# A new account of tiling changes in a kernel's planner, a freer place for eight scalings, and a refitted order: windowed attention followed by a four-expert mixture

## The chip, the cores and the metric

The kernel runs on one core of one Trainium2 chip. A core has five engines that run their own streams of instructions: TensorE (PE in the profile; its weight loads are listed as PEld), VectorE (DVE), ScalarE (ACT), GpSimd (POOL) and SyncE (SP). The metric is the device time of one execution in microseconds (us). Three runs of the kernel before took 358.85, 358.95 and 359.42 us; the median is 358.95.

## The reference

First an attention with "sink" keys and a short window: every query sees the first four keys and the 128 keys that end at itself. Then a mixture of four experts, each a pair of matrix products, weighted by normalised probabilities of the token.

```python
B, H, S, D = 4, 8, 768, 64          # n_sink 4, window 128
scores = scale * np.matmul(q, k.transpose(0, 1, 3, 2))
rel = pos[:, None] - pos[None, :]
keep = (pos[None, :] < n_sink) | ((rel >= 0) & (rel < window))
scores = np.where(keep, scores, -1000000000.0)
a = np.exp(scores - np.max(scores, axis=-1, keepdims=True))
a = a / (np.sum(a, axis=-1, keepdims=True) + 1e-09)
x = np.matmul(a, v).transpose(0, 2, 1, 3).reshape(B * S, H * D)   # 3072 x 512

p = domain_probs / (domain_probs.sum(-1, keepdims=True) + 1e-09)  # 3072 x 4
for e in range(4):                  # w1[e] 512 x 1024, w2[e] 1024 x 512
    h = np.maximum(x @ w1[e], 0.0)
    out += p[:, e:e + 1] * (h @ w2[e])
```

## The kernel before

**Attention.** Operands of TensorE are bf16, sums fp32 in PSUM. The four batches `b` are cut into three output groups `g` of 256 tokens and four pairs of heads `hp`. For a group, L706 makes the scores of a pair of heads (keys on the partitions, only the blocks inside the window), ACT takes the exponential into `aT` (L746), DVE multiplies by the window's mask (L754 in the first batch, L727 later; for `g` 0 of the first batch the mask is added in PSUM by products with `low` instead, L700). The sink keys' scores are L667, of 32 rows each. L779 (sinks) and L786 (window) multiply by the values into a PSUM tile `od` of 65 columns per head, the last of them the sum of the weights. DVE takes its reciprocal `R` (L813), and `od` times `R` is written to `onat`. For the first batch DVE does that in one instruction of 256 columns (L816); for the later batches ACT does it in four of 64 columns (L825, `multiply`). A bank of PSUM that holds `od` comes free when this is done.

The mixture needs tokens on the columns, so `onat` is turned to `xT`: by TensorE and a copy for the first batch (`turn`, L847), by one transposing DMA on SP's queue per group later (L803), issued behind the last of the group's four scalings. Rows of q and k are turned to `qkT` by TensorE in the first batch (L595, L598, copies L302) and by transposing DMAs on SP (L281) later. POOL issues the loads of rows (L271), values (L331) and weights.

**Mixture.** The first two groups of the first batch (`DENSE`) are done plainly: L1106 for `x @ w1` and L1433 for the second product, each collected by DVE with the gate as a column. All other groups save products: both matrix products are split into two by two blocks and done with seven block products instead of eight, so sums of operands and of results come in. For the first product these are

- `T`: four differences of blocks of `xT`, made by DVE in `tokens` (L1158), one after the other, each put off to a later place by a slack in ns;
- four forms of each expert's `w1` and `w2` (`weight_form1`, `weight_form`, L369 to L410), also DVE's;
- seven products P1, P5, P6, P2, P7, P3, P4 of 8 matmuls of 128 columns (L1189, `emit_fast`), whose PSUM tiles are copied, added to and finished by ACT and DVE (L1232, L1239, L1245, L1254), ending in `gated` (L1223), which takes relu and multiplies by a row of gates. P1 starts two PSUM tiles; where the second has not been wholly written since its last use as another shape (`unset`), a matmul of 512 columns writes it first.

The second product goes through the same seven (`CHAIN`), 4 matmuls of 256 columns for each expert and product (L1358, `emit_product`), with sums `S` of `H` (DVE, as `chore`), into two accumulator banks. After P1 its bank is copied to the other accumulator by ACT (L1387); DVE and ACT collect the rest into `osb` (L1390 to L1405), which SP stores.

The gates as rows are made once in `gates_by_row` (L462 to L468: four small DVE operations and a store to a tile in DRAM, `gate_rows`); `load_gate` (L485) broadcasts a row of it to all partitions. The planner places this when its clock passes `GROW`.

**The order.** Nothing reorders the instructions on the chip; the Python program that writes the kernel plans the order. It keeps a clock `t` for each engine, advanced by modelled costs (`pe`, `act`, `dve`, `pool`, `sp`), and a time at which each of six PSUM banks comes free. In the main loop it lists what PE could do next (a step of attention, a first product, a second product, a dense one), with the time each is ready and a priority number, and emits one. Work for DVE and ACT is put in a list by `later(engine, ready, slack, run)`; `flush` gives a free engine, among the entries that are ready, the one with the earliest due time (ready plus slack). An entry marked "any" goes to DVE or ACT, whichever the clock has free first. Where the clock sees PE without work for more than 220 ns, `idle_products` (L574) fills in a matmul of 256 columns of zeros. The constants at the top (`SHARE_OF`, `LEAD`, `LOW_PRODUCT`, `GATE`, `FORM`, `TOKEN` and so on) are slacks, priorities and the pace at which a later batch's attention is mixed into the experts' products. The modelled cost of a PE step has 95 ns for a change between tile sizes of the array: before, two such changes (`switch=2`) are charged to each step that uses small tiles, at its start, whatever came before or comes after.

Of the kernel before, what the change touches and what calls it, by code (L numbers as in the profile page):

```python
# [16 lines left out]
def kernel(  # L17
# [12 lines left out]
    nc = tc.nc  # L30

    B, H, S, D = q.shape
# [5 lines left out]
    P = 128  # L38
# [23 lines left out]
    DENSE = 2  # L62
    NT3 = 3
    MIX = 4
    SHARE_OF = (0.634, 1.111, 1.102)
    LEAD = (1.272, 0.235)
    DUE = 0
    LOW_PRODUCT = 2.791
    LOW_SECOND = 4.402
    HIGH_PRODUCT = 0.207  # L70
    EARLY = 0.154
    GATE = 8921
    GATE0 = 5401
    FORM = 20576
    FORM2 = 37391
    TOKEN00 = 33179
    TOKEN0 = 1119
    WAIT2 = 16164
    WAIT1 = 5898
    LATE3 = 3  # L80
    TOKEN = 11155
    MARGIN = 494
    FULL = 7
    STEP0 = 0.141
    READY = 46
    WIDE = 2
    OPEN = 1.198
    ONACT = 1
    ONE = 2
    PAIR = 1  # L90
    SINK2 = 1
    PAD = 198
    MASKD = 99999999
    GROW = 24662
    ONLY2 = 1
    BEHIND = 7198
    CHORES = 2
    OWN = 2
    BIASED = 1
    FAST = tuple(START)  # L100
# [7 lines left out]
    t = {"pe": 1200.0, "act": 0.0, "dve": 0.0, "pool": 1280.0, "sp": 800.0, "sw": 6500.0, "hw": 0.0}  # L108
    ring, whole = [0.0] * 6, [False] * 6
    WARM = 6600.0  # L110
    FLIP = 421
    LATE = 259
    LATE1 = 12449

    def pe(cols, *deps, n=1, switch=0):
        t["pe"] = max([t["pe"], *deps])
        rate = 2.4 if t["pe"] > WARM else 1.2
        t["pe"] += cols / rate + 2.5 * n + 95 * switch
        return t["pe"] + 215

    def act(cols, *deps):
# [41 lines left out]
    def later(engine, ready, slack, run):  # L163

        pend.append((ready, ready + slack, engine, run))
# [80 lines left out]
    qkn_free, scored_at = [0.0] * NQB, {}  # L246
# [334 lines left out]
    def transposes(b, g, hp):  # L581

        if b not in qkT:
            qkT[b] = sb.tile([P, 2, NHP, S], BF16, name="qkT", tag="qkT", bufs=1)
        ready = max(cast_at[hp // 2] if (b, g) == (0, 0) else rows_at(b, g), free_at(2 if (b, g) == (0, 0) else 1))
        slots, trs = [], []
        for i in range(2 if (b, g) == (0, 0) else 1):
            slots.append(pick())
            trs.append(bank(slots[i], [P, 2, 2, P], BF16, "tr"))
            ring[slots[i]] = 1e12  # L590
        hs = slice(2 * hp, 2 * hp + 2)
        for i in range(2):
            for tt in range(2):
                if (b, g) == (0, 0):
                    nc.tensor.transpose(trs[i][:, i, tt], first["qk"[i]][:, tt, hs], ident)  # L595
                    continue
                for ph in range(2):
                    nc.tensor.transpose(  # L598
                        trs[0][64 * ph:64 * ph + 64, i, tt], nat[b, 2 * g + i][:, 2 * hp + ph, tt * D:(tt + 1) * D], ident,
                    )  # L600
        done = pe(4 * P, ready, n=4, switch=0 if (b, g) == (0, 0) else 2)
        dst = qkT[b][:, :, hp, g * G:(g + 1) * G]

        def copied(at):
            for slot in slots:
                take(slot, at)
            turned_at[b, g, hp] = at

        if (b, g) == (0, 0):
            part = join(2, copied)  # L610
            for i, engine in enumerate(("dve", "act")):
                def run(engine, i=i):
                    copy(engine, dst[:, i].rearrange("c (p t) -> c p t", t=2), trs[i][:, i].rearrange("c t p -> c p t"))
                    part(clock(engine, 2 * P))
                later(engine, done, 0, run)
        else:
            def run(engine):
                copy(engine, dst.rearrange("c i (p t) -> c i p t", t=2), trs[0].rearrange("c i t p -> c i p t"))
                copied(clock(engine, 4 * P))
            later("any", done, 300, run)  # L620
        if hp == NHP - 1:
            for _ in range(2):
                qkn_free.remove(1e12)
                qkn_free.append(done)
            qkn_free.sort()
# [32 lines left out]
    def sinks(b, piece, n=1, joined=False):  # L658

        if b not in sinkA:  # L660
            sinkA[b] = sb.tile([P, 2 * G], BF16, name="sinkA", tag="sinkA", bufs=1)
        q0, q1 = piece * G, (piece + n) * G
        ready = 0.0 if joined else sinks_ready(b, piece, n)
        slot = pick()
        sp = bank(slot, [P, 2 * G], FP32, "sinks")
        for hp in range(NHP):
            nc.tensor.matmul(  # L667
                sp[32 * hp:32 * hp + 32, 0:q1 - q0], lhsT=ksd[b % 2][:, hp, :],
                rhs=qkT[b][:, 0, hp, q0:q1], start=True, stop=True,
            )  # L670
        done = pe(q1 - q0, 0.0 if joined else ready, switch=0 if joined else 2)
        ring[slot] = 1e12

        def run(engine):
            nc.scalar.activation(
                out=sinkA[b][:, q0 - G:q1 - G], in_=sp[:, 0:q1 - q0], func=AF.Exp, scale=scale,
            )
            at = act(q1 - q0)
            take(slot, at)
            for i in range(n):  # L680
                sinkA_at[b, piece + i] = at
        later("act", done, 800, run)
# [4 lines left out]
    def scores(b, hp, g, more=False):  # L687
        T = qkT[b]
        w = sum(x[2] for x in GROUPS[g]) * P
# [13 lines left out]
        for (kb, qb, nq) in GROUPS[g]:  # L703
# [6 lines left out]
                    start=not biased and c == 0, stop=True, skip_group_check=True,  # L710
                )
            c += nq * P
        scored_at[b] = done = pe(w, ready, n=6, switch=0 if more else 2)
        a = sb.tile([P, 2, w], BF16, name="aT", tag="aT", bufs=4)
        m = mask0 if g == 0 else mask1

# [46 lines left out]
    def values(b, hp, g):  # L763
# [33 lines left out]
        def scaled(at):  # L797
            take(slot, at)
            onat_at[b, hp, g] = at
            onat_n[b, g] = onat_n.get((b, g), 0) + 1  # L800
            if b and onat_n[b, g] == NHP:
                xT[b, g] = sb.tile([P, 2, NHP, P], BF16, name="xT", tag=home(b, g), bufs=1)
                nc.sync.dma_start(  # L803
                    out=xT[b, g].rearrange("c q h p -> c (q h) p"),
                    in_=o.rearrange("p q h c -> p (q h c)"), transpose=True,
                )
                turned_out = sp(at, issue=1330, takes=1400, turning=True)
                for x in range(NHP):
                    xT_at[b, x, g] = turned_out

        def run(engine):
            R = sb.tile([P, 2, 2, 1], FP32, name="R", tag="R", bufs=6)
            nc.vector.reciprocal(out=R, in_=od[:, :, :, D:DX])  # L813
            at = dve(4, fixed=171)
            if b < ONACT:
                nc.vector.tensor_mul(  # L816
                    o[:, :, hp].rearrange("p q (h d) -> p q h d", h=2), od[:, :, :, 0:D], R.to_broadcast([P, 2, 2, D]),
                )
                scaled(dve(2 * P))
                return  # L820

            def multiply(engine):
                for qi in range(2):
                    for ph in range(2):
                        nc.scalar.mul(o[:, qi, hp, ph * D:(ph + 1) * D], od[:, qi, ph, 0:D], R[:, qi, ph])  # L825
                        at = act(D)
                scaled(at)
            later("act", at, 600, multiply)
        later("dve", done, 500, run)
        values_at[b, g] = done  # L830

# [141 lines left out]
    class Mixture:  # L973
# [164 lines left out]
        def tokens(self):  # L1138

            pairs = [(b, g) for b in range(B) for g in range(NG) if any(self.is_fast(b, g, e) for e in FAST)]  # L1140
            n = len(self.T)
            if n == len(pairs):
                return
            b, g = pairs[n]
            if n >= NT3 and any((*pairs[n - NT3], e) not in self.finished for e in range(E)):
                return
            at = max(xT_at.get((b, hp, g), 1e12) for hp in range(NHP))
            if at > t["pe"] or t["pe"] < TOKEN00:
                return
            at = t["pe"]  # L1150
            x = xT[b, g]
            B11, B21, B12, B22 = x[:, 1, 0:2], x[:, 1, 2:4], x[:, 0, 0:2], x[:, 0, 2:4]
            T = sb.tile([P, 4, 2, P], BF16, name="T", tag="T", bufs=NT3)
            self.T[b, g] = {"P1": B11, "P2": B21, "P3": B22, "P4": T[:, 3], "P5": T[:, 0], "P6": T[:, 1], "P7": T[:, 2]}
            steps = [(T[:, 0], B12, B11), (T[:, 1], B22, T[:, 0]), (T[:, 2], B22, B12), (T[:, 3], B21, T[:, 1])]

            def run(engine):
                nc.vector.tensor_sub(*steps.pop(0))  # L1158
                done = dve(G, rate=1.92)
                if steps:  # L1160
                    later("dve", t["dve"], 1500 if b else TOKEN0, run)
                else:
                    self.T_at[b, g] = done
            later("dve", at, TOKEN if b else TOKEN0, run)

        def emit_fast(self, u, m, ready):
            b, g, e = u["unit"]
# [437 lines left out]
```

## Time and profile before

| | us | share of the span | instructions |
|---|---|---|---|
| profiled execution | 358.95 | | |
| its span | 357.2 | | 11108 |
| `cps` products, L1189, share of the chain | | 35% | |
| `acc` products, L1358, share of the chain | | 31% | |
| scalings L825 on ACT, busy | 32.8 | 9% | 144 |
| gated products L1223 on DVE, busy | 69.8 | 20% | 105 |
| exponentials L746 on ACT, busy | 46.5 | 13% | 96 |

The profiled execution took as long as the median of the three runs, so sums made against it can be read against the median. The span, 357.2 us, is the stretch in which the engines worked; 1.75 us of the time lie around it. Shares of the busy time don't tell which engine sets the end; the chain of waits (the work that ended last, followed back step by step) does. The engines' busy times overlap each other.

### The profile page before, as it was taken

How to read it: one execution, taken by the hardware profiler on the slowest of the kernel's cores; microseconds unless marked ns; L12 is line 12 of the kernel's file. 1: busy time of each engine (PE TensorE's matmuls, PEld its weight loads, DVE VectorE, ACT ScalarE, POOL GpSimd, SP SyncE). 2: the span in 40 equal slices, each digit the busy share in tenths (PEclk: the TensorE clock that was granted, in tenths of full speed). 3: DMA queues.
4: the chain of work that ended last, by engine and by line, in shares of the span. 5: the costliest groups of instructions: out<-in, count | busy, mean ns of one | idle time of the engine just before them, and what ended most of it. 6: DMA issues, size and time to landing. Idle time of an engine off the chain costs nothing.

```text
span 357.2 us, 11108 instructions
## 1 busy us (share of the span) xinstructions
PE 348.8 (98%) x4673; PEld 302.6 (85%) x4673; DVE 306.7 (86%) x701; ACT 168.7 (47%) x432; POOL 70.5 (20%) x90
## 2 busy tenths in 40 slices
PE   8999999999999999999999999999999999999995
PEld 3675687777688998998998998899899999999884
DVE  6669999998799899899699799699799699999630
ACT  5866451437882922566444722926443632322110
POOL 8934114311260440420030620000000000000000
PEclk9999999999999999999999999999999999999999
DMA  9999999999993999691086999124112221100011
GB/s 175 185 195 203 230 210 174 137 135 139 227 148 42 138 168 157 75 119 46 32 68 111 148 156 139 50 54 55 44 32 63 59 52 51 37 31 31 1 61 60
DMA packets 115318, 37.86 MB, mean 106 GB/s; under 512 B 97196, under 2 KB 110764, under 8 KB 115268
## 3 DMA queue, kind: packets, MB, share of 16 engines
q0 software_dynamic: 74416, 17.31, 55.4%
q1 hardware_dynamic: 39796, 19.32, 29.3%
q8 instruction: 36, 0.59, 0.7%
q10 hardware_dynamic: 1056, 0.52, 0.6%
q14 instruction: 14, 0.11, 0.1%
HBM read 41.03 MB, written 6.34 MB: 133 GB/s over the span
## 4 chain that ended last, share of the span: by engine, by line
PE 83%; DVE 6%; ACT 5%; DMA 2%; issue 1%; POOL 1%; DVEq 0%
PE cps L1189 35%; PE acc L1358 31%; PE acc L1433 7%; PE hps L1106 3%; PE sps L706 3%; ACT onat L825 2%; PE od L786 2%; ACT aT L746 2%; DMA vx<-in_v_dram 2%; DVE H L1223 1%; DVE cps L1239 1%; DMA gates<-gate_rows 1%; PE od L779 1%; DVE onat L816 1%; DVE H L1254 1%
## 5 line engine op out<-in xcount | busy, mean ns | idle before, releaser
L1189 PEld LDWEIGHTS <-w 128*128 128x128 bf16 x1408 | 87.1, 98 | 3.5 <-issue 1.0
L1358 PEld LDWEIGHTS <-H 128*128 128x128 bf16 x720 | 66.6, 98 | 7.9 <-issue 1.2
L1223 DVE SCALAR_TENSOR_TENSOR H<-cps,gates 128x512 bf16<-128x512 f32 x105 | 69.8, 683 | 0.0
L1358 PE MATMUL acc<-w,H 128*128 128x256 bf16 x432 | 56.8, 273 | 0.1
L1189 PE MATMUL cps<-xT,w 128*128 128x128 bf16 x704 | 52.5, 219 | 0.5 <-ACT onat L825 0.5
L1189 PE MATMUL cps<-T,w 128*128 128x128 bf16 x704 | 52.5, 219 | 0.1
L746 ACT ACTIVATE aT<-sps 128x512 bf16<-128x512 f32 (+1 forms) x96 | 46.5, 571 | 9.7 <-PE sps L706 9.5
L1232 ACT COPY cps<-cps 128x512 f32<-128x512 f32 x44 | 25.7, 592 | 44.2 <-PE cps L1189 33.8
L1405 ACT COPY osb<-acc 128x256 f32<-128x256 f32 x40 | 15.4, 384 | 59.2 <-PE acc L1358 59.2
L825 ACT ACTIVATE onat<-od,R 128x64 bf16<-128x64 f32 x144 | 32.8, 349 | 21.7 <-DVE R L813 21.7
L1358 PE MATMUL acc<-wf,H 128*128 128x256 bf16 x288 | 39.3, 273 | 0.0
L1189 PEld LDWEIGHTS <-qkn 128*128 128x128 bf16 x576 | 34.8, 98 | 1.1 <-issue 0.2
L1239 DVE TENSOR_TENSOR cps<-H,cps 128x512 f32<-128x512 f32 x40 | 27.7, 691 | 9.0 <-PE cps L1189 6.2
L1358 PEld LDWEIGHTS <-S 128*128 128x128 bf16 x320 | 30.2, 98 | 4.2 <-issue 1.0
L1245 ACT COPY H<-cps 128x512 f32<-128x512 f32 x40 | 23.7, 600 | 18.1 <-PE cps L1189 18.1
L1433 PE MATMUL acc<-w,H 128*128 128x512 bf16 x128 | 30.1, 379 | 0.0
L1189 PEld LDWEIGHTS <-vf 128*128 128x128 bf16 x480 | 28.8, 98 | 0.1
L331 POOL DMA_DIRECT2D vx<-in_v_dram x24 | 21.4, 909 | 37.4 <-PE od L786 25.9
L1254 DVE TENSOR_TENSOR H<-H,cps 128x512 f32<-128x512 f32 x40 | 27.0, 680 | 1.7 <-PE cps L1189 1.6
L271 POOL DMA_DIRECT2D rows<-in_q_dram x18 | 16.0, 887 | 61.1 <-DMA qkT<-rows 51.0
L1189 PE MATMUL cps<-T,qkn 128*128 128x128 bf16 x384 | 27.3, 219 | 0.1
L727 DVE TENSOR_TENSOR aT<-aT,mask 128x1024 bf16<-128x1024 bf16 (+1 forms) x36 | 22.8, 641 | 1.9 <-ACT aT L746 1.6
(123 smaller groups left out, 524.2 us busy)
## 6 DMA issues: line engine op xcount, KB each, us to landing
w<-in_moe_w_dram POOLq DMA_DIRECT2D x7, 1024.0 KB, 23.1
out_dram<-osb SPq DMA_DIRECT2D x23, 256.0 KB
gates<-gate_rows SPq DMA_DIRECT2D x40, 128.0 KB
vx<-in_v_dram POOLq DMA_DIRECT2D x24, 128.0 KB, 10.0
rows<-in_q_dram POOLq DMA_DIRECT2D x18, 128.0 KB, 6.4
rows<-in_k_dram POOLq DMA_DIRECT2D x18, 128.0 KB, 6.7
w<-in_moe_w_dram POOLq DMA_DIRECT2D x4, 256.0 KB, 8.4
kraw<-in_k_dram ACTq DMA_DIRECT2D x2, 256.0 KB
```

What stands on the lines that cost most here:

```text
L331: nc.gpsimd.dma_start(out=vx[tb][:, :, 0:D], in_=v[b, :, tb * P:(tb + 1) * P, :].rearrange("h p d -> p h d"),)
L727: nc.vector.tensor_mul(x, x, m[:, None, :].to_broadcast([P, n, 2 * w // n]))
L746: nc.scalar.activation(out=a[:, ph], in_=sps[ph][:, 0:w], func=AF.Exp, scale=scale)
L825: nc.scalar.mul(o[:, qi, hp, ph * D:(ph + 1) * D], od[:, qi, ph, 0:D], R[:, qi, ph])
L1189: nc.tensor.matmul(y[:, f], lhsT=A[:, d, f * P:(f + 1) * P], rhs=T[:, d], start=(m in ("P1", "P5") and f == 0 and d == 0), stop=(d == 1), ...
L1223: nc.vector.scalar_tensor_tensor(out=dst, in0=src, scalar=0.0, in1=gate, op0=ALU.max, op1=ALU.mult)
L1232: nc.scalar.copy(out=tiles["Y"], in_=y)
L1239: nc.vector.tensor_add(tiles["V"], c5, tiles["X"])
L1245: nc.scalar.copy(out=c5, in_=y)
L1254: nc.vector.tensor_add(c5, c5, y)
L1358: nc.tensor.matmul(x, lhsT=self.operand(b, g, e, m)[:, f], rhs=forms[e][m][:, f], start=(k == 0 and f == 0 and m in (("P1", "P5", "P2") if ...
L1433: nc.tensor.matmul(op, lhsT=H[:, fb // QF, fb % QF, s], rhs=w2_sb[e][:, fb, :], start=(fb == 0), stop=(fb == NFB - 1),)
```

## The change

The changed kernel computes the same thing. Four things are changed in the planner:

1. `pe` takes the number of rows of the step's tiles (128, 64, 65 for scores, 32 for sinks) and adds 95 ns where it differs from the step before. A tiling change is thus charged where it happens, also when a step of full tiles comes behind small ones, and not at all between steps of one kind.
2. For the second batch's first two output groups, (b, g) below `EITHER` = (1, 2), the scaling of `od` may run on DVE (as in the first batch, one instruction) or on ACT (four), whichever the clock has free first.
3. The four sums `T` of the second batch's first group get the slack `TOKEN1` (544 ns) instead of `TOKEN` (11155 ns) for the first and 1500 ns for the rest; and the time at which the planner believes that this group's `xT` has landed is at most `TURN1` (8645 ns) after its last scaling.
4. Some thirty constants have other values.

```diff
-    SHARE_OF = (0.634, 1.111, 1.102)
-    LEAD = (1.272, 0.235)
+    SHARE_OF = (0.909, 1.101, 1.118)
+    LEAD = (1.223, 0.045)
...
-    LOW_PRODUCT = 2.791
-    LOW_SECOND = 4.402
-    HIGH_PRODUCT = 0.207
-    EARLY = 0.154
-    GATE = 8921
-    GATE0 = 5401
-    FORM = 20576
-    FORM2 = 37391
-    TOKEN00 = 33179
-    TOKEN0 = 1119
-    WAIT2 = 16164
-    WAIT1 = 5898
+    LOW_PRODUCT = 2.173
+    LOW_SECOND = 3.131
+    HIGH_PRODUCT = 0
+    EARLY = 0.129
+    GATE = 6941
+    GATE0 = 7604
+    FORM = 13638
+    FORM2 = 49917
+    TOKEN00 = 25720
+    TOKEN1 = 544
+    TURN1 = 8645
+    TOKEN0 = 4051
+    WAIT2 = 15049
+    WAIT1 = 9563
     LATE3 = 3
-    TOKEN = 11155
-    MARGIN = 494
-    FULL = 7
-    STEP0 = 0.141
-    READY = 46
+    TOKEN = 13631
+    MARGIN = 0
+    FULL = 8
+    STEP0 = 0.122
+    READY = 0
     WIDE = 2
-    OPEN = 1.198
+    OPEN = 0.21
     ONACT = 1
+    EITHER = (1, 2)
...
-    PAD = 198
+    PAD = 208
     MASKD = 99999999
-    GROW = 24662
+    GROW = 32046
     ONLY2 = 1
-    BEHIND = 7198
-    CHORES = 2
+    BEHIND = 2768
+    CHORES = 1
...
-    FLIP = 421
-    LATE = 259
-    LATE1 = 12449
-
-    def pe(cols, *deps, n=1, switch=0):
-        t["pe"] = max([t["pe"], *deps])
+    FLIP = 809
+    LATE = 3730
+    LATE1 = 10389
+
+    tiling = [P]
+
+    def pe(cols, *deps, n=1, rows=P):
+        t["pe"] = max([t["pe"], *deps]) + 95 * (rows != tiling[0])
+        tiling[0] = rows
         rate = 2.4 if t["pe"] > WARM else 1.2
-        t["pe"] += cols / rate + 2.5 * n + 95 * switch
+        t["pe"] += cols / rate + 2.5 * n
         return t["pe"] + 215
...
-        done = pe(4 * P, ready, n=4, switch=0 if (b, g) == (0, 0) else 2)
+        done = pe(4 * P, ready, n=4, rows=P if (b, g) == (0, 0) else 64)
...
-        done = pe(q1 - q0, 0.0 if joined else ready, switch=0 if joined else 2)
+        done = pe(q1 - q0, 0.0 if joined else ready, rows=32)
...
-        scored_at[b] = done = pe(w, ready, n=6, switch=0 if more else 2)
+        scored_at[b] = done = pe(w, ready, n=6, rows=65)
...
                 turned_out = sp(at, issue=1330, takes=1400, turning=True)
+                if (b, g) == (1, 0):
+                    turned_out = min(turned_out, at + TURN1)
...
             def multiply(engine):
+                if engine == "dve":
+                    nc.vector.tensor_mul(
+                        o[:, :, hp].rearrange("p q (h d) -> p q h d", h=2), od[:, :, :, 0:D], R.to_broadcast([P, 2, 2, D]),
+                    )
+                    scaled(dve(2 * P))
+                    return
                 for qi in range(2):
...
-            later("act", at, 600, multiply)
+            later("any" if (b, g) < EITHER else "act", at, 600, multiply)
...
-                    later("dve", t["dve"], 1500 if b else TOKEN0, run)
+                    later("dve", t["dve"], TOKEN1 if (b, g) == (1, 0) else 1500 if b else TOKEN0, run)
...
-            later("dve", at, TOKEN if b else TOKEN0, run)
+            later("dve", at, TOKEN1 if (b, g) == (1, 0) else TOKEN if b else TOKEN0, run)
```

## The prediction

> **What bounds the kernel now.** I read the page's busy table, slices and chain first, then the trace by windows and in order of time, and last the starts of the 4673 matmuls one after another.
>
> ```profile
> PE 348.8 (98%) x4673; PEld 302.6 (85%) x4673; DVE 306.7 (86%) x701; ACT 168.7 (47%) x432; POOL 70.5 (20%) x90
> ...
> PE   8999999999999999999999999999999999999995
> ...
> PEclk9999999999999999999999999999999999999999
> ...
> PE 83%; DVE 6%; ACT 5%; DMA 2%; issue 1%; POOL 1%; DVEq 0%
> ```
>
> TensorE (PE) is busy in every slice, at full clock, and is 83% of the chain. So the time is PE's own work plus the places where PE stands. A matmul of 128 columns starts 56 ns after the one before (32 in 1.79 us on the chain), one of 256 columns 109 ns (40 in 4.37), and a change between tile sizes of the array costs about 98 ns more (93 to 99 ns at nearly all changes without a wait). Comparing each matmul's start with that spacing gives PE's waits. Those over 50 ns sum to about 7.4 us after the first 5.5 us: 3.2 in the head up to 24 us (first batch), 0.45 at the four fp32 transposes of L956, 0.6 from 30 to 34 us, 3.1 in all the rest. That is all that a better order can win. The largest single place:
>
> ```profile
> 100.00:104.00 4.00, 3.25 (x54) 2.86 (x52) 3.96 (x15) 4.00 (x20) 3.99 (x5) 1.00 2.22 141
> ```
>
> That is the table by windows for 100 to 104 us (the second batch's second output group); behind the length stand PE, weight loads, VectorE (DVE), ScalarE (ACT), POOL: ACT works 4.00 of 4 us and DVE 3.96. In order of time, PE and ACT there (start, length, instructions, idle time before and who ended it):
>
> ```profile
> 101.39 0.29 PE L786 MATMUL od<-vx,aT 128*128 128x65 bf16 x4 [0.26 <-DVE aT L727]
> 101.74 1.86 ACT L825 ACTIVATE onat<-od,R 128x64 bf16<-128x64 f32 x8
> 102.83 0.61 PE L1189 MATMUL cps<-xT,w 128*128 128x128 bf16 x8 [0.49 <-ACT onat L825]
> ```
>
> PE waits first for a mask that stands behind other DVE work, then for a PSUM bank that ACT's scalings (L825) still hold. By starts these cost 0.43 and 0.66 us, with 0.11 us for L825 at 95.1 us: 1.2 us here.
>
> **The change part by part.** The issue clock, the constants and the two new rules all act through one thing, the order in which the instructions are issued; so I compare the built orders of both kernels. The arithmetic is the same: 2464 product matmuls at L1189, 1120 at L1358, 128 at L1433, 128 at L1106. In the changed order PE has seven matmuls more: five idle fillers of 256 columns, all in the head, 5 x 0.109 = 0.55 us, and two seeds of 512 columns (the `unset` branch, before none; both are among full products, after 100 us) at 0.22 us (L1433, same width: 8 in 1.83) = 0.44. Tiling changes go from 66 to 68: 2 x 0.098 = 0.20, one of them in the head. So PE gets 1.2 us more work, and the waits must pay for it.
>
> **Head.** Up to the first product of output group 1, PE has 0.65 us more to issue (fillers, one tiling change). I walked the chains with the rows' durations: reciprocal 0.18 and scaling 0.42 on DVE, two exponentials 0.87 on ACT, bank copies 0.38 to 0.6, and the first expert's weight quarters, landed at 14.6, 16.8, 18.3 and 19.5 us. The fillers stand mostly where PE would stand anyway; the last wait (od, reciprocal, scaling, transpose L847, 0.83 us at 22.77) stays. I get that product at 23.1 us instead of 22.89: +0.2. If the fillers had no cover it would be +0.65, if they hid wholly 0.
>
> Behind it, the first batch's last transposes (L598) are followed at once by scores that need their copies: waits of 0.22 and 0.28 us at 30.42 and 30.94, on copies of 0.6 us. The new order puts eight matmuls of L1106 (0.87 us) between; only a wait of about 0.1 us for the last copy, queued on DVE behind the four small gate operations, is left: -0.4. These (L462 to L465) move from the head to just behind the second product's scaling, so `gate_rows` is written near 31.7 us instead of 23.8. It landed 9.5 us after its issue, and the first gate row 6.0 us after its own: 47.3 us now, against a first use (the first L1223, 50.24 us before) near 49.8. Covered by 2.5 us, where 10.8 were.
>
> **Second batch's first outputs.** Four of the eight scalings go to DVE: 16 ACT instructions of 0.21 us from start to start (16 in 3.38) leave, -3.4 us of ACT, and four of DVE's at 0.42 us (row L816) come, 0.35 us each with overlap, +1.4 us of DVE in a stage where it has 1.3 and 2.7 us idle in the 8 us windows before 100. The four sums T of group 0 now stand among them, and product units of that group start between the last values matmuls instead of behind all of them. What is left there by the same walk is 0.05 us for the banks of the score matmuls and 0.3 us for the copy of the first product P1 to the other accumulator (L1387, 0.37 us, which now has four matmuls of cover). Between 0 and 0.5 us comes on top where T waits for its transposed input (below); I take 0.25. So 1.2 becomes 0.6: -0.6.
>
> **Later.** The same comparison of consumer and producer, place by place: 65.0/65.6 us (products behind weight forms on DVE) 0.39 to 0.28; 82 to 85 us, 0.38, unchanged; 124.2 (behind twelve L825) 0.27 to 0.14; 160.3 (product straight after the P1 copy) 0.23 to 0; 173 and 176 (L825 again) 0.15 to 0; 228.0 (sink scores behind L825) 0.29 to 0.1; the last, 330.0 and 330.6, the same sequence in both: unchanged, as is the chain of thirteen L1358 groups behind it. Together -0.11 - 0.13 - 0.23 - 0.15 - 0.19 = -0.8. Seeds and one tiling change add 0.44 + 0.10 = +0.54.
>
> **Sum.** +0.2 - 0.4 - 0.6 - 0.8 + 0.54 = -1.06 us on the profiled execution of 358.95 us (span 357.2, 1.7 around it), which is also the median: 357.9. What the walk can't see goes both ways. A wait that is new because an engine is a little later than its row says: there are some fifteen places whose margin is under 0.1 us, a few tenths in all. All removed waits real and no other: -1.6. I say 357.8, own range 356.8 to 358.5.
>
> The moves past the queues: on SP, the last two key transposes of the second batch now go before the first output stores, and xT of group 0 stands behind two stores as before. On POOL the third batch's vx loads move ahead of its later rows; each still has over 20 us to its reader. For the other xT transposes the distance from last scaling to first T grows (group 1: 8.8 to 10.9 us, group 2: 11.9 to 14.8), at no cost.
>
> **Rivals.** (1) *T blocks DVE: slower.* T's first subtraction stands on DVE's queue and waits for the transposed xT. Behind it stand a scaling, a mask, the next reciprocals, and all of these feed PE.
>
> ```profile
> 95.08 1.24 SPq L803 DMA_TRANSPOSE xT<-onat  x1
> ...
> 103.63 1.27 SPq L803 DMA_TRANSPOSE xT<-onat  x1
> ...
> 123.40 1.26 SPq L803 DMA_TRANSPOSE xT<-onat  x1
> ```
>
> By the semaphores these three landed at 98.17, 109.76 and 131.49 us: 3.1, 6.1 and 8.1 us. The first ran just before the row loads that POOL issues from 96.11 us on, the others among loads. T has 3.9 us after the last scaling in the new order (3.5 before, when it just sufficed: T started 0.5 us after the landing). At 6.1 us the mask for the third values group ends 6.1 + 0.20 + 0.35 + 0.20 + 0.69 = 7.5 us after the scaling, and PE wants it at 5.4: 2.1 us of standing, 1.9 more than I took. Then 357.8 + 1.9 = 359.7, and at 8.1 us 361.7; about 3.5 us is what I counted, 5.3 us makes the change worth nothing. For it: the last key transpose is no longer behind the stores, so it can land near 94 us instead of 95.5, and the row loads that wait for it start earlier, perhaps into this transfer. Against: the transfer itself starts near 93 us, two us earlier. Chance 0.14.
>
> The Trainium skill (Advanced Engine Details and Errata, X-Bar Transpose) has transposing DMAs as fast as regular ones. By that rule xT would land as the plain store issued at 96.38 did, 2.98 us later, and the time would be 357.6. The trace agrees for the first transfer (3.1) and not for the next two (6.1, 8.1). The skill's DMA: Bandwidth & Descriptors (Arbitration) says that an engine takes turns between the queues it has work for, which speaks for the rows as the cause and keeps this rival.
>
> (2) *The order trades waits for waits: no change.* PE's 1.2 us more work is sure; the walk's -1.8 us of waits after the head is not. If half comes, the sum is +0.2 - 0.9 + 0.54 = -0.2: 358.8. For it: DVE is at 19.9 of 20 us from 60 to 80 and 20.0 from 300 to 320, so any wait saved can reappear there. Against: before 100 us DVE has room, and the removed places differ in cause. Chance 0.15.
>
> (3) *Gates late: slower.* If `gate_rows` and the first gate row take 5 us more than the 15.5 they took, DVE stands 2.5 us at its first gated product, with the seven weight forms behind; PE can live on the six PSUM banks for less than 1 us, so 357.8 + 1.6 = 359.4 or more. Chance 0.04. (4) *Small new waits in DVE's full stretches* (forms now ordered by other due times): ten of 0.25 us make 357.8 + 2.5 = 360.3. Chance 0.05.
>
> **How the numbers follow.** The forecast has 0.62, the rivals 0.38. About 0.2% (0.7 us) is what a measurement of this kernel can tell from no change: faster is under 358.2, slower over 359.7. The forecast's upper end and rival 2 give the middle; rival 1 falls half over its edge, more at 8 us. Faster 0.64, same 0.16, slower 0.20. The range takes the forecast, rival 2, and the lower part of the slower cases: 356.5 to 360.1.
>
> **What would show it.** Fillers 26, no wait at the scores behind L598, PE in the two output groups of the second batch standing under 0.7 us instead of 1.2, ACT no longer full there, DVE's T starting within 0.5 us of its turn; xT's landing within 3.5 us of its issue. Wrong is the forecast if DVE stands over 1 us before that T or before the first gated product, or if waits of PE after 110 us sum to more than 1.5 us (now 1.2).

## The result and the profile after

The changed kernel takes 360.36 us in the median of 6 runs (359.99 to 360.78), the kernel before 359.09 us (358.55 to 359.42): a ratio of 1.0037, 95% interval 1.0024 to 1.0049. It is slower by 1.3 us, where 357.8 us were forecast; the time lies just outside the stated range of 356.5 to 360.1 us. The profiled execution took 360.50 us, its span 358.8 us. From the page, in the order in which the lines of before were shown:

```profile
PE 348.7 (97%) x4671; PEld 302.2 (84%) x4680; DVE 306.4 (85%) x703; ACT 166.2 (46%) x418; POOL 68.8 (19%) x90
...
PE   8989999999979999999999999999999999999995
...
PE 90%; DMA 3%; DVE 3%; ACT 1%; POOL 1%; issue 1%; DVEq 0%
```

PE's own time is as before. One slice of PE's row, that from 99 to 108 us, has fallen to 7, and the one from 18 to 27 us from 9 to 8 (the head, see below). (The kernel issues 4680 matmuls; nine records are missing.) The chain of waits by line has a newcomer, `DMA out_dram<-osb` with 2%. The table by windows for the stretch that was shown of before, and the one behind it (length, PE, weight loads, DVE, ACT, POOL):

```profile
100.00:104.00 4.00, 3.08 (x55) 2.86 (x52) 0.84 (x3) 2.55 (x9) 2.27 (x3) 1.00 2.23 166
104.00:108.00 4.00, 2.54 (x43) 2.43 (x44) 4.00 (x12) 0.58 (x1) 0.00 (x0) 1.00 1.99 117
```

ACT is no longer full (2.55 us where it was 4.00), as forecast. But DVE, which worked 3.96 of the first four microseconds before, works 0.84: it stands. In order of time, DVE (start, length, instruction, idle time before it and what ended it):

```profile
97.34 0.26 DVE L1172 TENSOR_TENSOR T<-xT 128x256 bf16<-128x256 bf16 x1
...
99.82 0.39 DVE L1318 TENSOR_TENSOR S<-H 128x512 bf16<-128x512 bf16 x1
103.38 0.43 DVE L1318 TENSOR_TENSOR S<-S,H 128x512 bf16<-128x512 bf16 x1 [3.16 <-DMA out_dram<-osb]
...
104.85 0.42 DVE L832 TENSOR_TENSOR onat<-od,R 128x256 bf16<-128x256 f32 x1
```

The first line is the first sum T, for which rival 1 feared: it runs without a wait. (In the changed kernel the lines of the second half stand 14 further: T is L1172, the sums S are L1318, L1189 is L1203, L1358 is L1372.) What waits, 3.16 us, is the second of the sums S, the operands of the second product. It waits for the store of an output tile to land. The reason is in the code of both kernels: the tile of the second dense group's output (`out_sb`, tag `wide1`) and the second tile of sums (`S1`, also `wide1`) share a buffer, so this S (below: S1) may not be written before that output has been read out. Behind it on DVE's queue stands the scaling at 104.85, and PE needs the bank that this scaling frees:

```profile
105.33 0.84 PE L1203 MATMUL cps<-T,vf 128*128 128x128 bf16 x12 [2.24 <-DVE onat L832]
```

By starts PE lost 2.41 us there. From the chain of waits in this stretch, start, length and what it was:

```profile
96.76 6.50 DMA out_dram<-osb
...
103.38 0.43 DVE S L1318
...
104.85 0.42 DVE onat L832
```

The store was issued at 96.76 us and landed 6.50 us later, where in the kernel before it was issued at 96.38 and landed at 99.36, 2.98 us later. There S1 was first written at 101.73 us, 2.4 us after that landing (from the rows of SP and DVE; `S<-H` is the other tile of sums, `S<-S,H` is S1):

```profile
96.38 0.56 SPq L1451 DMA_DIRECT2D out_dram<-osb  x1
...
99.80 0.73 DVE L1304 TENSOR_TENSOR S<-H 128x512 bf16<-128x512 bf16 x2
...
101.73 0.42 DVE L1304 TENSOR_TENSOR S<-S,H 128x512 bf16<-128x512 bf16 x1
```

So two things came together. The new order wants S1 straight behind the first S, at 100.2 us, 1.5 us earlier than before: had the store taken 2.98 us again, it would have landed at 99.74, 0.5 us before that. And the store took 3.5 us longer. What changed beside it is the start of the third batch's row loads, before and now:

```profile
96.11 0.88 POOL L271 DMA_DIRECT2D rows<-in_q_dram  x1 [0.39 <-ACT aT L746]
...
94.39 0.88 POOL L277 DMA_DIRECT2D rows<-in_q_dram  x1 [0.39 <-ACT aT L752]
```

They come 1.7 us earlier, since the key transpose that they wait for moved ahead of the output stores on SP (issued at 90.02 instead of 91.60 us). Their first packets moved at 98.3 us before, when most of the store's packets had gone, and at 96.1 now, 2.6 us before the store's first packet (98.8). Of the 16 parts of the store, 15 were in at 101.08 us and the last at 103.26: all parts were late, as the loads make them (e2), and one part was later still by 2.2 us (e3 and the last section).

Apart from this place the order came out, in sum, near what was forecast. Without these 2.41 us, PE's waits over 40 ns fell from 9.5 to 7.5 us (some 2 us of both lie in the first 5.5 us), against 1.15 us of added work.

### The profile page after: what moved, and what is told of

It is laid out like the page before. It is cut to its first block, busy times and chain, and to the rows that moved or that the text cites. A ratio compares the mean times of both kernels' runs of the same rounds, so it can differ in the third digit from the quotient of the medians.

```text
span 358.8 us, 11099 instructions
## 1 busy us (share of the span) xinstructions
PE 348.7 (97%) x4671; PEld 302.2 (84%) x4680; DVE 306.4 (85%) x703; ACT 166.2 (46%) x418; POOL 68.8 (19%) x90
## 4 chain that ended last, share of the span: by engine, by line
PE 90%; DMA 3%; DVE 3%; ACT 1%; POOL 1%; issue 1%; DVEq 0%
PE cps L1203 37%; PE acc L1372 34%; PE acc L1447 7%; PE hps L1120 3%; PE sps L712 3%; PE od L792 2%; DMA out_dram<-osb 2%; DMA vx<-in_v_dram 2%; PE od L785 1%; DVE onat L824 1%; PE tr L604 1%; DVE cps L1253 1%; PE sinks L673 0%; PE acc L580 0%; DVE aT L760 0%
## 5 line engine op out<-in xcount | busy, mean ns | idle before, releaser
L1203 PEld LDWEIGHTS <-w 128*128 128x128 bf16 x1408 | 87.2, 98 | 3.1 <-issue 0.4
L1372 PEld LDWEIGHTS <-H 128*128 128x128 bf16 x740 | 68.4, 98 | 7.7 <-issue 1.0
L1237 DVE SCALAR_TENSOR_TENSOR H<-cps,gates 128x512 bf16<-128x512 f32 x108 | 71.5, 679 | 0.1
L1372 PE MATMUL acc<-w,H 128*128 128x256 bf16 x444 | 58.5, 273 | 0.1
L1203 PE MATMUL cps<-T,w 128*128 128x128 bf16 x704 | 53.1, 219 | 0.2
L1203 PE MATMUL cps<-xT,w 128*128 128x128 bf16 x704 | 52.5, 219 | 0.0
L1372 PE MATMUL acc<-wf,H 128*128 128x256 bf16 x296 | 40.0, 273 | 0.0
L1253 DVE TENSOR_TENSOR cps<-H,cps 128x512 f32<-128x512 f32 x41 | 28.2, 689 | 12.0 <-PE cps L1203 10.8
L1203 PEld LDWEIGHTS <-qkn 128*128 128x128 bf16 x576 | 34.7, 98 | 0.9
L839 ACT ACTIVATE onat<-od,R 128x64 bf16<-128x64 f32 x128 | 29.2, 354 | 12.0 <-DVE R L821 12.0
L1372 PEld LDWEIGHTS <-S 128*128 128x128 bf16 x320 | 30.2, 98 | 4.5 <-issue 1.1
L1203 PEld LDWEIGHTS <-vf 128*128 128x128 bf16 x480 | 28.6, 98 | 2.7 <-DVE onat L832 2.4
L1447 PE MATMUL acc<-w,H 128*128 128x512 bf16 x119 | 28.8, 379 | 0.6 <-issue 0.2
L1203 PE MATMUL cps<-T,qkn 128*128 128x128 bf16 x384 | 27.2, 219 | 0.0
L1203 PE MATMUL cps<-T,vf 128*128 128x128 bf16 x320 | 22.3, 219 | 2.2 <-DVE onat L832 2.2
L1237 DVE SCALAR_TENSOR_TENSOR H<-H,gates 128x512 bf16<-128x512 f32 x36 | 24.4, 680 | 0.0
```

What stands on the lines that cost most here:

```text
L1203: nc.tensor.matmul(y[:, f], lhsT=A[:, d, f * P:(f + 1) * P], rhs=T[:, d], start=(m in ("P1", "P5") and f == 0 and d == 0), stop=(d == 1), ...
L1237: nc.vector.scalar_tensor_tensor(out=dst, in0=src, scalar=0.0, in1=gate, op0=ALU.max, op1=ALU.mult)
L1253: nc.vector.tensor_add(tiles["V"], c5, tiles["X"])
L1372: nc.tensor.matmul(x, lhsT=self.operand(b, g, e, m)[:, f], rhs=forms[e][m][:, f], start=(k == 0 and f == 0 and m in (("P1", "P5", "P2") if ...
L1447: nc.tensor.matmul(op, lhsT=H[:, fb // QF, fb % QF, s], rhs=w2_sb[e][:, fb, :], start=(fb == 0), stop=(fb == NFB - 1),)
```

## The experiments

Theory A: the loss is S behind the store, and the store is late because the row loads came forward (A1), or because of an instruction packet (A2, A3), a DMA packet of 16 KB that the profile calls "instruction" (see e3). Theory B is rival 1 as predicted, T behind its transposed input. All times are medians beside runs of the kernel before on the same chip, which were 358.9 to 359.1 us.

**e1, the output tile in a buffer of its own.** Order and instructions are the same; only the shared buffer is gone.

```diff
-                out_sb[g] = mo.tile([P, 2, Dout], FP32, name="osb0", tag=f"wide{g}" if g < 2 else "osb", bufs=1)
+                out_sb[g] = mo.tile([P, 2, Dout], FP32, name="osb0", tag="wide0" if g < 1 else "osb", bufs=1)
```

> The changed kernel, same order of every engine, but the second dense output tile (out_sb of group 1) lies in the buffer osb instead of wide1, which the sums S also use. Theory A (the loss is VectorE's 3.16 us of standing at 103.38 us, where the sum S may not overwrite the buffer before the store of that output tile has landed; PE stands 2.41 us for the scaling L832 queued behind): that standing is gone, 360.4 - 2.3 = 358.1 us, PE's largest wait after 60 us under 0.4 us. Theory B (rival 1 as predicted: T waits for the transposed xT, or the wait only moves to what is next on VectorE): no change, 360.4 us within 0.4.

Measured 358.82 us, ratio 0.9993 (0.9983 to 1.0004), in two groups: six runs at 358.12 to 358.48, six at 359.17 to 359.55. The lower group is theory A's number; none of its runs was profiled. The profiled execution (359.17) is of the upper one, and DVE shows a reason:

```profile
97.24 0.18 DVE L821 RECIPROCAL R<-od 128x4 f32<-128x4 f32 x1
98.58 0.29 DVE L1172 TENSOR_TENSOR T<-xT 128x256 bf16<-128x256 bf16 x1 [1.16 <-DMA xT<-onat]
```

S no longer waits, but T does, 1.16 us. In this execution the row loads went out at 92.96 us, 1.4 us earlier than in the profile above, and xT's transfer was slow: 5.1 us from issue to landing (93.44 to 98.55) instead of 3.1. PE stood 0.41 and 0.74 us for it. So both theories name a real wait; A is the larger and B the one behind it.

**e2, the row loads later.** Twelve more copies of two columns on POOL ahead of the third batch's row loads; the planner's clock isn't told.

```diff
-                nc.gpsimd.tensor_copy(out=held, in_=qkT[b][:, 1, NHP - 1, S - 2:S])
+                for _ in range(13 if b == 1 else 1):
+                    nc.gpsimd.tensor_copy(out=held, in_=qkT[b][:, 1, NHP - 1, S - 2:S])
```

> The changed kernel with twelve more two-column copies on POOL between the second batch's last key transpose and the third batch's row loads, so that these are issued about 2 us later (near 96.5 us instead of 94.39). Theory A1 (the store lands late because the row loads take the transfer engines before it): the store issued at 96.76 lands about 3 us after its issue, near 99.8 us, before the instruction packet at 100.5; no standing of S, 358.1 us. Theory A2 (the store is late for another reason, the instruction packet alone): it still lands after 102 us, 360.4 us.

Measured 357.99 us (357.77 to 358.24), ratio 0.9968 (0.9957 to 0.998). The loads went out at 98.69 us, 4.3 us later rather than 2, and the store landed at 100.11 us, 2.9 us after its issue. An instruction packet fell at 97.73 us in this execution and made it 0.9 us late; it had landed all the same when S came. The two stretches of the windows' table:

```profile
100.00:104.00 4.00, 4.00 (x71) 3.92 (x70) 3.96 (x13) 2.98 (x12) 4.00 (x6) 1.00 1.71 109
104.00:108.00 4.00, 4.00 (x64) 3.86 (x62) 3.93 (x9) 0.93 (x2) 2.56 (x3) 1.00 2.07 172
```

PE works 8.00 of 8 us and DVE 7.89. PE's waits sum to 7.7 us. This shows A1: with the loads out of the way the store is in time, although a packet fell into it, and the loss is gone. It is also the version that beats both kernels, by 0.9 us against before. S1 began here at 100.66 us, so even now the margin is some 0.5 us.

**e3, the instruction packet moved.** In the first profile of the changed kernel one part of the store came 2.2 us after the other 15; a packet of 16 KB of the kind "instruction" had begun at 100.53 us and taken 1.12 us. The warm-up products and seventeen matmuls of the dense second product were cut into smaller ones, for 160 instructions more on PE without a column more.

```diff
-    idle_products(acc[1], 9)
+    for _ in range(9 * 8):
+        nc.tensor.matmul(acc[1][:, 0:64], lhsT=zeros[:, 0:P], rhs=zeros[:, 0:64], start=True, stop=True)
...
-                nc.tensor.matmul(
-                    op, lhsT=H[:, fb // QF, fb % QF, s], rhs=w2_sb[e][:, fb, :],
-                    start=(fb == 0), stop=(fb == NFB - 1),
-                )
+                for c in range(halves):
+                    cs = slice(c * Dout // halves, (c + 1) * Dout // halves)
+                    nc.tensor.matmul(
+                        op[:, cs], lhsT=H[:, fb // QF, fb % QF, s], rhs=w2_sb[e][:, fb, cs],
+                        start=(fb == 0 and c == 0), stop=(fb == NFB - 1), skip_group_check=True,
+                    )
```

> The changed kernel with its warm-up products cut into pieces of 64 columns and seventeen dense products into two halves: 80 matmuls more, no column more, so that PE's instruction packets of 16 KB come at other places (by count of instructions near 94.5 and 101.5 us instead of 100.53). Theory A3 (one transfer engine carries the packet for 1.1 us, is 2.2 us late after it, and the store waits for this one engine: 15 of its 16 parts were in at 101.08, the last at 103.26): the store lands near 101.1 us, VectorE stands 1 us instead of 3.2, PE about 0.2 us; 358.2 to 358.6 us. Theory A1 alone (row loads): it lands at 103.3 still, 360.4 us.

Measured 359.20 us, but spread from 357.84 to 361.69 over 12 runs, ratio 1.0007 (0.9985 to 1.0028). The profiled execution (357.91) is theory A3's: packets at 92.85 and 102.58 us, the store in with all 16 parts at 100.40, S waiting 0.20 us. But the row loads went out at 95.55 us in it, 1.2 us later than in the first profile, so it fits A1 as well. Five runs lie at 357.8 to 358.0, five over 360, and these five have no profile. Inconclusive for the time; how far the packet makes one part late is seen in other profiles too (last section).

**e4, the control of e1.** The kernel before with the same line changed.

> Control: the kernel before with the same buffer moved as in e1. There the store landed at 99.36 us and S began at 99.80 without a wait, so all theories expect no change: 358.9 us within 0.4. If it gains over 0.5 us, the buffer frees something else and e1 is no proof.

Measured 359.36 us, ratio 1.0013 (1.0002 to 1.0024): no gain; it is slower by 0.4 us, 0.06 us outside what was expected, with two of twelve runs over 360 us. The buffer frees nothing else. (The S that began at 99.80 us is the other tile of sums; S1 was first written at 101.73 us.)

**e5, the control of e2.** The kernel before with the same twelve copies.

> Control: the kernel before with the same twelve copies on POOL as in e2, so that the row loads come about 2 us later than 96.11 us. Theory A1 (in the kernel before the transposed xT and the store had landed before the loads mattered, 98.17 and 99.36 us): no change, 358.9 us within 0.4. Rival (later row loads help any order, so that e2's gain is not the changed kernel's own): 358.2 us or less.

Measured 358.90 us, ratio 0.9998 (0.9989 to 1.0007): no change, with the loads at 101.62 us, 5.5 us later than before. Later row loads help only the changed order.

**e6, without the freer scaling.** e2 with `EITHER = (0, 0)`.

> e2 (the changed kernel with later row loads, 357.99 us) with EITHER = (0, 0): all scalings of the second batch on ACT again, everything else as changed. If the freer scaling is what emptied the second batch's first groups (theory), ACT is full there again, PE stands some 0.4 to 0.8 us for banks that hold od, 358.4 to 358.8 us. If the rest of the new order did it (rival), 358.0 us within 0.2.

Measured 362.04 us (360.66 to 362.62 in four runs, the profiled one 362.62), 4.1 us slower than e2, far more than either number. Two things make up most of it. ACT is full: from 92 to 96 us PE works 3.06 of 4 us, DVE 0.75 and ACT all of it,

```profile
92.00:96.00 4.00, 3.06 (x26) 1.37 (x25) 0.75 (x1) 4.00 (x19) 2.40 (x13) 1.00 0.33 121
```

and PE stands 0.25, 0.60 and 0.49 us at the score banks and the sink scores. And since the last scalings end later, xT goes out at 95.31 us instead of 93.85 and the store at 98.27 instead of 97.17. The row loads went out at 96.19 us, 2.5 us earlier than in e2 (the key transpose before them was issued 1.2 us earlier, and the thirteen copies took 3.13 us instead of 4.42), so they are ahead of the store again:

```profile
104.54 0.42 DVE L1318 TENSOR_TENSOR S<-S,H 128x512 bf16<-128x512 bf16 x1 [2.80 <-DMA out_dram<-osb]
```

PE lost 2.20 us by that; most of the rest is 0.38 us at 101.63 us and 0.84 us from 123 to 126. Here 15 parts of the store were in 5.6 us after its issue and the last 0.5 us behind them, so nearly all of this lateness is in all parts and not in a single one. The freer scaling is worth its place by the 1.3 us at the banks; how much of the 4.1 us is its own can't be said, since the loads moved too.

**e7, the sums T on their old slacks.** e2 without `TOKEN1` and `TURN1`.

> e2 with the four sums T of the second batch's first group on the old slacks (TOKEN for the first, 1500 ns for the rest) and without TURN1; EITHER as changed. If the early sums matter by themselves: PE comes to the products with T before the sums are made or has them later in the order and stands 0.3 to 0.6 us more, 358.3 to 358.6 us. If they only use up VectorE's room: 358.0 us within 0.2.

Measured 358.32 us (358.12 to 358.47), ratio 0.9978 (0.9969 to 0.9988), 0.3 us over e2: at the edge of what was expected of the first theory, and the interval overlaps that of e2. The waits of the second batch are no larger than in e2; what is added stands at 130.9 and 133.1 us (0.15 and 0.37 us, products of the next groups).

**e8, the two rules alone.** The kernel before with the freer scaling, early T and `TURN1`, its own constants and its own account of tiling changes.

> The kernel before with the two new rules for the second batch alone (scaling on either engine, sums T at once with TURN1), its own constants and its own account of tiling changes; no more matmuls than before. If the rules remove most of the 1.08 us that PE stood in these groups and no transfer gets in the way: 358.0 to 358.4 us. If T or S meets a transfer as in the changed kernel, 359.2 us or more; then VectorE's standing shows which.

Measured 359.50 us, ratio 1.0012 (1.0003 to 1.0021). The profiled execution is the longest of the ten (360.41). Here T waits for its transfer:

```profile
99.98 0.29 DVE L1166 TENSOR_TENSOR T<-xT 128x256 bf16<-128x256 bf16 x1 [0.62 <-DMA xT<-onat]
```

This time it is not the row loads: they were issued at 97.97 us, and their first packets moved at 99.87. xT, issued at 95.77 us right behind a store (95.00 to 98.61), landed at 99.95, after 4.2 us instead of 3.1. The mask behind T is late, and PE stands 1.52 us before the second batch's next values products (L786 at 102.19). In this execution the 1.08 us that the rules save are given back at once.

**e9, without the fillers.** e2 with the seventeen idle matmuls of the head left out, same order otherwise.

```diff
-            idle_products(acc[1], 1, G)
+            pe(G)
```

> e2 (357.99 us) without the seventeen idle matmuls that the planner puts into the head (17 x 0.109 = 1.85 us of PE); the order of all else is the same. If they stand where PE would stand anyway (the prediction's term for the head): 358.0 us within 0.3, the waits of the head growing by what the fillers took. If they have no cover: 356.2 us. By the excess of the head (0.65 us worse than forecast): 357.3 us.

Measured 358.09 us: no change. PE's waits up to 20 us rose from 4.10 to 5.61 us, which is most of the 1.85 us that the fillers take. The fillers cost nothing.

**e10, both covers.** e1 and e2 together.

> The changed kernel with both: the second dense output tile in its own buffer (e1) and the row loads 2 us later (e2). If e2 already took away all standing behind transfers: 358.0 us within 0.2, as e2. If S still met the store in some executions of e2: 357.7 us or less.

Measured 358.17 us (358.07 to 358.57), as e2: with the loads out of the way, nothing is left for the other buffer to win.

**e11, the changed kernel again.**

> The changed kernel once more, for a second profiled execution. Theory A: the row loads go out near 94.4 us again, and VectorE stands 2 to 3.5 us in all at S behind the store, at T behind xT, or at both; PE loses 2 to 2.6 us there; 360.4 us. If the standing of the first profile was an accident of that execution: 358.1 us.

Measured 360.32 us, ratio 1.0027 (1.0017 to 1.0038). The row loads went out at 94.04 us. DVE shows both waits in one execution:

```profile
97.87 0.29 DVE L1172 TENSOR_TENSOR T<-xT 128x256 bf16<-128x256 bf16 x1 [0.30 <-DMA xT<-onat]
...
103.08 0.43 DVE L1318 TENSOR_TENSOR S<-S,H 128x512 bf16<-128x512 bf16 x1 [2.30 <-DMA out_dram<-osb]
```

PE lost 0.30 and 1.77 us. The store (issued at 96.91) landed at 102.96, its other 15 parts at 101.75.

**e12, the new account of tiling changes alone.** The kernel before with the new `pe` and nothing else.

> The kernel before with the new account of tiling changes alone, its own constants and rules: one matmul of 256 columns and two tiling changes more (0.3 us). If the truer clock alone makes the better order after 110 us and before 90 us: 358.4 us. If constants fitted to the old clock don't suit it: 359.3 to 360 us.

Measured 367.81 us, ratio 1.0243 (1.0216 to 1.027): far worse than both numbers. PE's waits sum to 17.0 us instead of 9.5, spread over the whole span (1.02 us at 50.9 us, 3.2 us from 100 to 120 us, 1.2 us from 160 and 1.5 us from 240 us on). A truer clock with constants fitted to the old one makes a poor order; the account and the constants can only be judged together. The new constants under the old account were not run, so what each of the two is worth stays open.

## Why the prediction was wrong

- **Added work, +1.2 us**: right. 0.96 us of columns and 0.19 us for two tiling changes.
- **Head, +0.2 us up to the first product of group 1**: mis-sized. That product came at 23.82 us instead of 22.89, +0.93: 0.65 us more work, and 0.3 us of waits on top (0.66, 0.30 and 0.48 us for scalings and their turning, where before it was 0.22 and 0.82). So the upper bound given there, +0.65, was too low. The fillers are not to blame: without them the product starts at 23.83 us in e9, with them at 23.75 in e10 and 24.23 in e2. The three waits are for scalings and turnings, so it is that chain which ends later in the new order.
- **Behind the head, -0.4**: right. The two waits at 30.42 and 30.94 us (0.49 us by starts) are gone. With the head's term, the first of the saving products (L1189) starts 0.51 us later than before (46.74 against 46.23 us), where 0.2 us earlier was forecast. `gate_rows` was issued at 32.93 us and landed at 41.86; the first gate row was in at 47.05, 3.7 us before the first gated product (50.74). Rival 3 did not happen.
- **Second batch, -0.6**: the part that was counted is right, and better by 0.35 us once T doesn't wait. What is left of the 1.2 us is 0.25 us at 99.46, behind the P1 copy (forecast at 0.3), and in e2 nothing else. The 0.29 us at 107.86 stand behind DVE's `cps` of L1253, which the collision made late; e2 has no such wait.
- **Later, -0.8 and +0.54**: right or a little better. The waits at 124.2, 160, 173, 176 and 228 us are gone, 0.13 us stand at a new place (135.5), the place at 65 us went from 0.38 to 0.26 us and that from 82 to 85 us from 0.38 to 0.22. After 110 us PE's waits over 50 ns sum to 0.5 us instead of 1.2, so rivals 2 and 4 did not happen.
- **The sum**: without the collision the new order runs at 357.99 us (e2), against 357.8 forecast and a range of its own of 356.8 to 358.5. That it meets so well is in part luck: the head came out 0.7 us worse, and the second batch and the later places together some 0.6 us better.
- **The step that failed** is the one on the transfers' queues: "on SP, the last two key transposes of the second batch now go before the first output stores", counted at nothing. Moving them ahead released the row loads 1.7 us earlier, and these delayed a store that an instruction on DVE waits for: 3.16 us on DVE, 2.41 us on PE, which with e2's 357.99 us gives the 360.4 measured. The walk of producers and consumers took each transfer to take as long as before, and does not list S1 among the consumers: in the new order it had 0.5 us to spare, where it had 2.4 us.
- **Rival 1** had the right kind of event ("the row loads that wait for it start earlier, perhaps into this transfer") and nearly its price (359.7 us), and it does happen: T waited 0.30 us in e11 and 1.16 in e1 with row loads about, and 0.62 in e8 without them. But it watched only xT. The store has a margin of its own, it is issued 3.3 us after xT and so lies deeper among the loads, and it decided. The chance of 0.14 was too low also because a second transfer on the same queue had the same danger.
- The two rules of the Trainium skill that were weighed: "DMA: Bandwidth & Descriptors", Queues, rings and completion order, under Arbitration (an engine takes turns between the queues that have work for it) is the one that fits better; both transfers were slow where row packets were there (xT 5.1 us in e1 against 3.1, the store 6.1 to 6.5 us in e6, e11 and after against 2.9 in e2), though e8's 4.2 us for xT came without them. The rule of the X-bar transpose ("Advanced Engine Details and Errata", X-Bar Transpose (TRN2)), that these transfers are as fast as plain ones, was read too far: 357.6 us came of it by taking a plain store that ran before the loads. The two slow transposes of the kernel before (6.1 and 8.1 us) took no longer than transfers issued beside them (a `vx` load at 103.05 us 5.9, a row load at 123.90 us 8.2), so they don't speak against the rule; it says nothing on what both take in a crowd.

## What to carry to other kernels

When an edit moves a transfer forward on its queue, list every transfer that is in flight in the next few microseconds and every instruction that waits for one of them, also those that wait because a buffer is shared; a margin of 0.5 us behind a 3 us store is none. An instruction that moves forward uses up such a margin as well as a transfer that comes late. A planner that orders by a clock needs the landing of a store under load as a term, not a constant. And where constants were fitted to a model, a more truthful model has to be tried with constants fitted again, and the two judged as one.

## What the runs showed beside that

An instruction packet seems to make transfers late. In each of the fourteen profiles a packet of 16,384 bytes of the kind "instruction" began between 92.8 and 102.6 us and took 0.9 to 1.6 us. In all but e5 and e9, where no other packets moved at that time, transfers that landed in the next microseconds had one part of 16 that came 0.5 to 2.2 us after the other fifteen, in several profiles until the row loads were through (after: 103.26 against 101.08 us for the store, then 1.6 to 2.1 us for six loads). In the profile after, these 2.2 us are the larger part of the 3.16 us that S1 waited; in e6 they were 0.5 of 2.80. The Trainium skill ("Runtime: NRT & Kernel Launch", Instruction fetch mechanics) has engines refill their instructions in blocks of 16 KiB by a DMA queue of their own, at a cost that is mostly hidden; the size agrees with the packets here; a transfer in flight does not seem to be spared. That the packet is the cause rests on its time in these profiles; e3, which meant to move it, did not settle it by the clock, and in e5 one load had a part 1.6 us late with no such packet near, only one of 8 KB.
